# Reordering the start of an attention and expert kernel: casts, clamps, register loads, idle products and value rows

## The chip, the cores and the metric

One Trainium2 chip, one core. The metric is device time in microseconds (us), the median of several executions. An execution is "fast" when it lies within 1.5% of the fastest of its kernel; all the profiled executions quoted here were fast, and all ratios use fast runs only. Times inside an execution are counted from the start of the profiled span; the whole time is about 1.8 us more than the span (335.48 against 333.7 for the kernel before in its profiled execution).

## The reference, cut to what matters

```python
def _attn_ref(q, k, v, global_idx):              # float32, 8 batches x 8 heads x 576 tokens x 64
    scores = 1.0 / np.sqrt(D) * np.matmul(q, k.transpose(0, 1, 3, 2))
    mask = np.abs(pos[:, None] - pos[None, :]) <= 32
    mask = mask | is_global[:, None] | is_global[None, :]     # 8 global tokens, the same for all heads
    scores = np.where(mask, scores, -1e9)        # then softmax over the last axis
    return np.matmul(attn, v)

def _moe_ref(x, w_in, w_out):                    # x 4608x512, w_in 512x2048, w_out 2048x512
    r = np.maximum(x @ w_in, 0.0)
    return (r * r) @ w_out
```

Attention is a band of 65 tokens plus 8 "global" tokens that attend to everything and are attended by everything. Its result, one row per token, goes through two dense products.

## The kernel before: the parts that the change and the argument touch

Everything is placed by hand: in the trace an engine's instructions come in the order of the program text (VectorE's clamps at 6.74 to 7.85 us and its register load at 7.70 to 8.55, then the casts of head pair 1 from 8.63), so where a line stands decides what it holds up. Batch 0 is done in two halves of 288 query columns. Its first half (`half0`) needs casts, TensorE transposes and masks; its second half (`half1`) is mixed with the first products of the expert part ("projections", `mm1_half`). From batch 2 on the kernel is a steady mixture of attention and dense products.

```python
    def clamped(t, off, top):                    # two VectorE instructions on 8 numbers
        dve.tensor_scalar(out=t, in0=g32, scalar1=off, scalar2=0, op0=ALU.add, op1=ALU.max)
        dve.tensor_scalar(out=t, in0=t, scalar1=top, scalar2=None, op0=ALU.min)

    def columns():
        clamped(g32a, 0, HS)
        clamped(g32b, -255, S - 256)
    ...
    def fetch_globals():                         # SyncE: rows of the global tokens
        ...                                      # batch 0's v rows into gv0, then
        for nm in "kqv":                         # batches 1 and 2: k rows, q rows, v rows
            for g in range(NG):
                nc.sync.dma_start(out=grow[nm][g : g + 1], in_=...)

    def globals_in_place():
        for nm in "kq":
            act.copy(out=nat[nm][TP : TP + NG, :, TJ - 1], in_=grow[nm][:, 0])
        dve.tensor_copy(out=g16s["v"], in_=grow["v"])
        ...
    def value_globals(b):                        # SyncE: v rows of the global tokens into the value tile
        for x in range(NT):
            nc.sync.dma_start(out=vb[b][0:NG, x, 0 : 2 * H : 2], in_=...)

    def tokens_to_scratch(b):                    # GpSimd issues: batch b's k and q as fp16 rows in HBM
        for nm in "kq":
            ...
            for x in range(n):
                pool.dma_start(out=scr[(nm, b % 2)][...], in_=src[nm][b, :, lo:hi].rearrange("h s d -> s h d"))
    ...
    def scatter(b, part=None, pairs=slice(0, NHP)):   # the global tokens' outputs over their columns
        ...
        for g in range(NG):                      # the column comes from a VectorE register
            dve.tensor_copy(
                out=xT[:, pairs, lo:hi][:, :, ds(gvs[part][g], 1)],
                in_=gxs[b][:, pairs, g : g + 1],
            )
    ...
    # the order of the program's start
    cast_tokens(dve.tensor_copy, "k", 0)
    cast_tokens(act.copy, "q", 0)
    mask_natural(0)
    transposes0(0)
    mg = mask_globals_matmul(0)
    mask_globals(mg, 0)
    columns()                                    # clamps and a register load on VectorE,
    load_columns(0)
    cast_tokens(dve.tensor_copy, "k", 1)         # ahead of the casts of head pair 1
    cast_tokens(dve.tensor_copy, "q", 1)
    ...
    take(SCHED["h1"])                            # projections of the first half of the tokens
    half1(2)
    half1(3)
    ...
    half1_out(3)
    scatter(0, 1)                                # the second half's scatter
    take(99)
    globals_in_place()
    value_globals(1)                             # batch 1's v rows: only here
    globals_to_scratch(2)
    tokens_to_scratch(2)
```

In the steady part, after the first unit of batch b, GpSimd copies one number computed by that unit (`pin`, a brake so that the transfers do not start too early), on some batches gathers the global rows, then issues batch b+1's tokens to scratch; SyncE transposes them into `qb` and `kb`, which batch b+1's scores read.

The softmax here doesn't subtract the row's maximum and nothing guards it: scores larger than these inputs give would overflow.

## Time and profile before

| | kernel before |
|---|---|
| time, median of 3 runs | 335.12 us (334.07 to 335.83) |
| profiled span | 333.7 us |
| mean granted TensorE clock | 0.974 |
| TensorE busy from 75 to 290 us | 213.9 of 215.0 us |

Parts of the page of the kernel before. The first rows give busy us of an engine, its share of the span and its number of instructions; `PEclk` is the granted TensorE clock in tenths, for 40 equal slices of the span (8.3 us each).

```profile
span 333.7 us, 6906 instructions
...
PE 319.6 (96%) x2418; PEld 168.4 (50%) x2418; DVE 230.7 (69%) x681; ACT 211.4 (63%) x417; POOL 106.2 (32%) x137
...
PEclk9659988999999999999999999999999999999999
```

TensorE (PE) is busy 96% of the span, so a change must either take work from it, fill its last holes, or end the stretches at half clock: slices 2 and 3, and 6 and 7, are below 9.

Two more views of the kernel before matter for what follows; the prediction did not show them. First the instructions of one tile: VectorE's (DVE) scatter copies over the whole execution, with the least, median and greatest duration in ns. Then the order of time around the second half's scatter: start, length, engine, line, operation, output<-input, and in brackets what the engine waited for.

```profile
L729 DVE COPY xT<-gx x72: 170/177/814, 25.6 to 274.1; 128x4 f16 x72
```

```profile
33.70 3.65 POOL L405 DMA_DIRECT2D scr_k<-in_k_dram  x4
...
34.91 2.79 PE L528 MATMUL mm<-xT,w_in 128*128 128x256 f16 x24
...
36.54 2.45 DVE L729 COPY xT<-gx 128x4 f16 x8
...
38.23 0.76 POOL L405 DMA_DIRECT2D scr_k<-in_k_dram  x1 [0.88 <-DMA w_out<-in_moe_w_out_dram]
...
39.05 1.92 PE L528 MATMUL mm<-xT,w_in 128*128 128x256 f16 x16 [0.66 <-DVE xT L729]
```

A scatter copy takes 177 ns, but one of them took 814. Eight undisturbed ones take 1.66 us with the steps between them (measured further below); this scatter took 2.45. Its first copy, of 814 ns, runs from 36.54 to 37.35, beside GpSimd (POOL) still issuing four scratch copies, and its last, of 338 ns, beside the issue at 38.23. TensorE waits 0.66 us for the scatter.

### The profile page before, as it was taken

The page shows a single profiled execution, that of the slowest core. Times are in us where ns is not written, and L with a number is a line of the kernel's source. Part 1 is how long each engine was busy: PE and PEld are TensorE (multiplying, and loading weights), DVE is VectorE, ACT ScalarE, POOL GpSimd, SP SyncE. Part 2 cuts the span into 40 slices and gives each one's busy share as a digit, 9 for nine tenths or more (in the row PEclk, how much of TensorE's full clock was granted, in tenths as well). Part 3 has the DMA queues.
Part 4 walks back from the last instruction along what each step waited for, and adds up shares of the span by engine and source line. Part 5 has one row for each costly group of instructions (what it writes and reads, how often), then busy time and mean ns, then how long its engine had stood idle before and what let it go on. Part 6 is the DMA issues. An engine that isn't in the chain of part 4 may idle for free.

```text
span 333.7 us, 6906 instructions
## 1 busy us (share of the span) xinstructions
PE 319.6 (96%) x2418; PEld 168.4 (50%) x2418; DVE 230.7 (69%) x681; ACT 211.4 (63%) x417; POOL 106.2 (32%) x137
## 2 busy tenths in 40 slices
PE   7888879999999999999999999999999999999995
PEld 2676755444454555455455445454545444444443
DVE  7686976888858885878588858885888584323511
ACT  4487765659954995399549954995499537404600
POOL 9545653005930593059004940590000000000000
PEclk9659988999999999999999999999999999999999
DMA  8999999922999399979952999999510001011011
GB/s 194 179 203 180 203 172 144 138 97 47 132 152 151 83 120 151 165 111 136 156 113 72 110 143 140 163 146 134 119 65 0 33 31 64 2 66 60 3 63 63
DMA packets 148716, 37.59 MB, mean 113 GB/s; under 512 B 136658, under 2 KB 144202, under 8 KB 148682
## 3 DMA queue, kind: packets, MB, share of 16 engines
q0 software_dynamic: 105168, 17.93, 70.6%
q1 hardware_dynamic: 43368, 19.10, 29.9%
q8 instruction: 19, 0.31, 0.4%
q10 hardware_dynamic: 146, 0.13, 0.1%
q14 instruction: 15, 0.12, 0.1%
HBM read 37.31 MB, written 17.05 MB: 163 GB/s over the span
## 4 chain that ended last, share of the span: by engine, by line
PE 77%; DMA 7%; DVE 7%; SPq 3%; ACT 3%; issue 2%; DVEq 0%
PE mm L509 25%; PE mm L572 24%; PE tr L509 9%; PE tr L572 5%; DMA qb<-scr_q 4%; PE sc L657 3%; PE acc L657 3%; PE sc L612 2%; DVE xT L729 2%; SPq L356 2%; DMA vb<-g16sv 2%; PE mm L528 2%; PE acc L612 1%; DMA grows<-in_k_dram 1%; DVE xT L710 1%
## 5 line engine op out<-in xcount | busy, mean ns | idle before, releaser
L572 PE MATMUL mm<-w_out,gt 128*128 128x512 f16 x448 | 104.5, 379 | 0.0
L509 PE MATMUL mm<-xT,w_in 128*128 128x512 f16 x384 | 90.1, 379 | 0.4 <-DVE xT L729 0.3
L572 PEld LDWEIGHTS <-gt 128*128 128x128 f16 x560 | 52.5, 98 | 58.5
L509 PEld LDWEIGHTS <-w_in 128*128 128x128 f16 x512 | 47.5, 98 | 53.4 <-issue 0.5
L514 ACT ACTIVATE rl<-mm 128x512 f16<-128x512 f32 x96 | 54.7, 600 | 25.6 <-PE mm L509 25.0
L515 DVE TENSOR_TENSOR gt<-rl 128x512 f16<-128x512 f16 x128 | 52.2, 423 | 16.5 <-ACT rl L514 14.4
L621 ACT ACTIVATE et<-sc 128x880 f16<-128x880 f32 (+1 forms) x32 | 28.9, 903 | 46.8 <-PE sc L612 46.8
L624 DVE TENSOR_TENSOR et<-et,mask 128x880 f16<-128x880 f16 (+1 forms) x64 | 38.9, 614 | 24.6 <-ACT et L621 23.4
L113 POOL DMA_DIRECT2D vb<-in_v_dram x40 | 41.1, 1594 | 6.1 <-DMA w_in<-in_moe_w_in_dram 5.1
L509 PE MATMUL tr<-xT,w_in 128*128 128x512 f16 x128 | 33.0, 380 | 0.0
L549 DVE COPY ot<-mm 128x512 f32<-128x512 f32 (+1 forms) x29 | 19.7, 680 | 17.5 <-PE mm L572 15.8
L871 POOL COPY pin<-gsh 1x1 f32<-1x1 f32 x5 | 0.9, 177 | 95.4 <-DVE gsh L698 95.4
L710 DVE TENSOR_TENSOR xT<-sc,rec 64x288 f16<-64x288 f32 (+1 forms) x55 | 25.0, 455 | 7.2 <-ACT rec L681 6.1
L681 ACT ACTIVATE rec<-rec 128x288 f32<-128x288 f32 x64 | 28.3, 443 | 2.0
L621 ACT ACTIVATE et<-acc 128x880 f16<-128x880 f32 (+1 forms) x32 | 29.0, 907 | 0.9 <-PE acc L612 0.9
L657 PEld LDWEIGHTS <-vb 128*128 128x128 f16 x288 | 21.3, 98 | 12.6 <-issue 1.8
L405 POOL DMA_DIRECT2D scr_k<-in_k_dram x30 | 26.7, 1114 | 1.7 <-DMA w_out<-in_moe_w_out_dram 0.9
L710 DVE TENSOR_TENSOR xT<-acc,rec 64x288 f16<-64x288 f32 (+1 forms) x55 | 25.0, 455 | 3.2 <-ACT rec L681 0.6
L680 ACT ACTIVATE rec<-sc 64x288 f32<-64x288 f32 (+1 forms) x55 | 22.4, 406 | 7.1 <-PE sc L657 4.2
L405 POOL DMA_DIRECT2D scr_q<-in_q_dram x24 | 24.8, 1582 | 5.2 <-DMA w_out<-in_moe_w_out_dram 5.1
L572 PE MATMUL tr<-w_out,gt 128*128 128x512 f16 x112 | 25.3, 379 | 0.0
L680 ACT ACTIVATE rec<-acc 64x288 f32<-64x288 f32 (+1 forms) x55 | 22.2, 404 | 1.3 <-PE acc L648 0.3
(146 smaller groups left out, 310.1 us busy)
## 6 DMA issues: line engine op xcount, KB each, us to landing
out_dram<-ot SPq DMA_DIRECT2D x35, 256.0 KB
vb<-in_v_dram POOLq DMA_DIRECT2D x32, 120.0 KB, 10.0
scr_q<-in_q_dram POOLq DMA_DIRECT2D x24, 144.0 KB, 6.2
scr_k<-in_k_dram POOLq DMA_DIRECT2D x24, 120.0 KB, 4.6
w_in<-in_moe_w_in_dram POOLq DMA_DIRECT2D x4, 512.0 KB, 13.4
w_out<-in_moe_w_out_dram POOLq DMA_DIRECT2D x4, 512.0 KB, 9.9
natk<-in_k_dram POOLq DMA_DIRECT2D x3, 288.0 KB, 14.0
natq<-in_q_dram POOLq DMA_DIRECT2D x3, 288.0 KB, 11.2
```

The lines of the kernel that those rows point to most:

```text
L113: pool.dma_start(out=vb[b][NG : NG + KN[x], x, 2 * hs.start : 2 * hs.stop : 2], in_=v[b, hs, x * KT : x * KT + KN[x]].rearrange("h s d -> ...
L405: pool.dma_start(out=scr[(nm, b % 2)][x * pitch + off : x * pitch + off + hi - lo].rearrange("s (h d) -> s h d", d=D), in_=src[nm][b, :, l ...
L509: nc.tensor.matmul(ph, w_in[:, t, u * P : (u + 1) * P], xT[:, t, XOFF + c * TC : XOFF + (c + 1) * TC], start=(t == 0), stop=(t == NDM - 1),)
L514: nc.scalar.activation(out=rl, in_=ph, func=AF.Relu)
L515: nc.vector.tensor_tensor(out=gts[c][:, u, :], in0=rl, in1=rl, op=ALU.mult)
L572: nc.tensor.matmul(po, gts[c][:, f, m * P : (m + 1) * P], w_out[:, f, :], start=(f == 0), stop=(f == NFF - 1),)
L621: act.activation(out=et[:, :, 0:W], in_=sc[:, :, 0:W], func=AF.Exp, bias=0.0, scale=scale)
L624: dve.tensor_tensor(out=et[:, :, 0:W], in0=et[:, :, 0:W], in1=mask[:, MB[half] : MB[half] + W].unsqueeze(1).to_broadcast((P, 2, W)), op=AL ...
L657: nc.tensor.matmul(banks[e][:, o : o + w], vtf[:, t, vo : vo + P], et[:, e, so : so + w], start=(n == 0), stop=(n == nw - 1), skip_group_c ...
L680: act.activation(out=rec[r], in_=av[xs][rs, :, 0:GTOK], func=AF.Ln)
L681: act.activation(out=rec, in_=rec, func=AF.Exp, scale=-1.0)
L710: dve.tensor_tensor(out=xT[r, hp, x0 : x0 + HS].rearrange("p (k x) -> p k x", k=2), in0=av[x][r, :, 0:GTOK], in1=rec[r], op=ALU.mult,)
```

## The change

The intent: take small work on VectorE out of the way of head pair 1's casts; make each clamp one instruction; put idle products into TensorE's waits so that the clock stays up (without them its mean was 0.972 to 0.984, with them 0.990 to 1.000, measured below); fetch and place batch 1's value rows before TensorE needs them.

```diff
-SCHED = dict(wa=6, w0=6, w1=5, w2=3, w3=2, w4=1, ...)
+SCHED = dict(w5=2, w6=1, w7=2, wa=6, w0=6, w1=5, w2=2, w3=4, w4=0, ...)
...
-    def clamped(t, off, top):
-        dve.tensor_scalar(out=t, in0=g32, scalar1=off, scalar2=0, op0=ALU.add, op1=ALU.max)
-        dve.tensor_scalar(out=t, in0=t, scalar1=top, scalar2=None, op0=ALU.min)
+    def clamped(t, least, most, of=None):
+        dve.tensor_scalar(
+            out=t, in0=g32c if of is None else of, scalar1=least, scalar2=most,
+            op0=ALU.max, op1=ALU.min,
+        )
...
-        for nm in "kqv":
+        for nm in "vkq":
...
+    def values_in_place():
+        dve.tensor_copy(out=g16s["v"], in_=grow["v"])
+        value_globals(1)
...
-        act.copy(out=gv16, in_=gv0)
+        dve.tensor_copy(out=gv16, in_=gv0)
...
-    cast_tokens(act.copy, "q", 0)
+    cast_tokens(dve.tensor_copy, "q", 0)
+    transposes0(0)
+    cast_tokens(dve.tensor_copy, "k", 1)
+    cast_tokens(act.copy, "q", 1)
     mask_natural(0)
-    transposes0(0)
-    mg = mask_globals_matmul(0)
-    mask_globals(mg, 0)
-    columns()
-    load_columns(0)
-    cast_tokens(dve.tensor_copy, "k", 1)
-    cast_tokens(dve.tensor_copy, "q", 1)
...
     half0(0)
+    keep_warm(SCHED["w5"])
     half0(1)
...
+    columns()
+    load_columns(0)
     v_globals()
...
     take(SCHED["h1"])
+    values_in_place()
     half1(2)
...
+    globals_in_place()
     scatter(0, 1)
     take(99)
-    globals_in_place()
-    value_globals(1)
+    next_in_place()
     globals_to_scratch(2)
     tokens_to_scratch(2)
```

Cut here: the same row copies split into three functions, the clamps' new bounds (the index base is moved into the access pattern instead of being subtracted), two further `keep_warm` calls and the mask's globals placed behind head pair 1's transposes. The arithmetic of the result is unchanged.

More of the change, by code (lines that the diff above doesn't have):

```diff
@@ L42 @@
 MB = (0, 456)
-SCHED = dict(wa=6, w0=6, w1=5, w2=3, w3=2, w4=1, h0=0, w=4, h1=3, h2=2, h3=0, p0=0, p1=2, p2=2, b1=((2, 1, 2), (2, 1, 2), (1, 1, 2), (2, 0, 4)))
+SCHED = dict(w5=2, w6=1, w7=2, wa=6, w0=6, w1=5, w2=2, w3=4, w4=0, h0=0, w=4, h1=3, h2=2, h3=0, p0=0, p1=2, p2=2, b1=((2, 1, 2), (2, 1, 2), (1, 1, 2), (2, 0, 4)))
 ONES = 2.0**-7 * (1.0 + 15360.0 / 2**23)
@@ L197 @@
     gbf = sbt("gbf", [P, NG], FP32)
-    g32, g32a, g32b, g32c = (sbt("g32" + x, [1, NG], I32) for x in ("", "a", "b", "c"))
+    g32a, g32b, g32c = (sbt("g32" + x, [1, NG], I32) for x in "abc")
     oh = sbt("oh", [P, NT, NG], FP16)
@@ L206, in indices @@
         low = g64.bitcast(I32).rearrange("p (g two) -> p g two", two=2)[:, :, 0]
+        clamped(g32c, 0, S - 1, low)
         nc.vector.tensor_copy(out=g16, in_=low)
@@ L209, in indices @@
         nc.tensor.matmul(gb, ones, g16, start=True, stop=True)
-        nc.vector.tensor_copy(out=g32, in_=low)
-        clamped(g32c, 0, S - 1)
-        return gb
-    def clamped(t, off, top):
-        dve.tensor_scalar(out=t, in0=g32, scalar1=off, scalar2=0, op0=ALU.add, op1=ALU.max)
-        dve.tensor_scalar(out=t, in0=t, scalar1=top, scalar2=None, op0=ALU.min)
+        return gb
+    def clamped(t, least, most, of=None):
[3 more added lines that the diff above has]
+        )
     def columns():
         clamped(g32a, 0, HS)
-        clamped(g32b, -255, S - 256)
+        clamped(g32b, 255, S - 1)
     def one_hots(gb):
@@ L368, in globals_in_place, with next_in_place @@
             act.copy(out=nat[nm][TP : TP + NG, :, TJ - 1], in_=grow[nm][:, 0])
-        dve.tensor_copy(out=g16s["v"], in_=grow["v"])
+    def next_in_place():
         for nm in "kq":
@@ L717, in load_columns @@
     def load_columns(part):
-        idx, top = {None: (g32c, S - 1), 0: (g32a, HS), 1: (g32b, S - 256)}[part]
+        idx, low, top = {None: (g32c, 0, S - 1), 0: (g32a, 0, HS), 1: (g32b, 255, S - 1)}[part]
         _, gvs[part] = nc.values_load_multi_w_load_instructions(
-            idx[0:1, 0:NG], engines=[mybir.EngineType.DVE], min_val=0, max_val=top,
+            idx[0:1, 0:NG], engines=[mybir.EngineType.DVE], min_val=low, max_val=top,
             skip_runtime_bounds_check_because="the values are clamped on the chip",
@@ L725, in scatter @@
         lo, hi = {
-            None: (XOFF + b * S, XOFF + (b + 1) * S), 0: (0, HS + 1), 1: (XOFF + 255, XOFF + S),
+            None: (XOFF + b * S, XOFF + (b + 1) * S), 0: (0, HS + 1), 1: (XOFF, XOFF + S),
         }[part]
@@ L748 @@
     cast_tokens(dve.tensor_copy, "k", 0)
-    cast_tokens(act.copy, "q", 0)
+    cast_tokens(dve.tensor_copy, "q", 0)
+    transposes0(0)
+    cast_tokens(dve.tensor_copy, "k", 1)
+    cast_tokens(act.copy, "q", 1)
     mask_natural(0)
-    transposes0(0)
-    mg = mask_globals_matmul(0)
-    mask_globals(mg, 0)
-    columns()
-    load_columns(0)
-    cast_tokens(dve.tensor_copy, "k", 1)
-    cast_tokens(dve.tensor_copy, "q", 1)
     keep_warm(SCHED["w3"])
     tr_k(1, tail=act.copy, last=act.copy)
+    mg = mask_globals_matmul(0)
     keep_warm(SCHED["w4"])
     tr_q(1, act.copy)
+    mask_globals(mg, 0)
     ets = {}
@@ L792 @@
         pool.dma_start(out=w_out[:, ts(j, 4), :], in_=wo[:, ts(j, 4), :])
+    columns()
+    load_columns(0)
     v_globals()
     half0(2)
+    keep_warm(SCHED["w6"])
     half0(3)
+    keep_warm(SCHED["w7"])
     half0_out(0, "mm")
```

## The prediction

> **What bounds the kernel now.** I read the page's row of slices first, then the stretches between the changes of the granted TensorE clock, then the first 75 us instruction by instruction. In the stretches view a row gives start:end, length, then busy us of each engine with its instruction count, the granted clock, the DMA share and GB/s (all times here are us from the span's start):
>
> ```profile
> core 0: us, PE busy (x) PEld busy (x) DVE busy (x) ACT busy (x) POOL busy (x), PEclk, DMA share, GB/s
> 4.25:11.07 6.82, 4.43 (x69) 2.86 (x68) 5.81 (x25) 2.73 (x12) 6.75 (x8) 0.98 1.54 202
> 11.07:24.73 13.66, 12.20 (x222) 9.70 (x222) 9.93 (x39) 9.96 (x24) 6.17 (x8) 0.51 1.44 197
> 24.73:48.62 23.89, 20.41 (x254) 15.18 (x253) 19.38 (x52) 16.85 (x33) 12.98 (x16) 0.99 1.66 186
> 48.62:52.03 3.41, 3.39 (x28) 2.27 (x29) 1.14 (x4) 1.75 (x4) 3.41 (x5) 0.54 2.29 168
> 52.03:75.00 22.97, 22.46 (x244) 11.62 (x242) 18.73 (x68) 13.14 (x28) 0.68 (x1) 1.00 1.11 124
> 75.00:333.70 258.70, 253.69 (x1601) 125.83 (x1599) 173.34 (x480) 165.74 (x319) 72.72 (x84) 1.00 0.90 97
> ```
>
> From 75 us on TensorE is busy 253.7 of 258.7 us at the full clock, and the diff leaves that part alone. So the change is worth whatever it moves the point at 75 us, and no more. Before it TensorE runs at half clock twice, 11.07 to 24.73 and 48.62 to 52.03. "Busy" there means slow, not well used. The two causes are in the order of time, VectorE then TensorE:
>
> ```profile
> 6.74 0.15 DVE L215 TENSOR_SCALAR g32a<-g 1x8 int32<-1x8 int32 x1
> 6.92 0.16 DVE L216 TENSOR_SCALAR g32a<-g32a 1x8 int32<-1x8 int32 x1
> 7.00 0.65 DVE L215 TENSOR_SCALAR g32b<-g 1x8 int32<-1x8 int32 x1
> 7.69 0.16 DVE L216 TENSOR_SCALAR g32b<-g32b 1x8 int32<-1x8 int32 x1
> 8.63 0.56 DVE L435 CAST nat0k<-stk 96x768 f16<-96x768 f32 x1 [0.79 <-DVE g32b L216]
> 9.11 0.74 DVE L435 CAST nat0q<-stq 96x768 f16<-96x768 f32 x1
> ```
>
> ```profile
> 9.25 0.43 PE L453 MATMUL mm<-identity,nat0k 96*128 96x96 f16 x6 [1.97 <-DVE nat0k L435]
> ...
> 46.63 0.26 PE L648 MATMUL sc<-et,vb 128*64 128x160 f16 x2 [0.44 <-DVE gt L540]
> 46.70 0.26 PE L648 MATMUL sc<-et,one 128*64 128x160 f16 x2
> 48.02 0.27 PE L648 MATMUL sc<-et,vb 128*64 128x192 f16 x2 [1.05 <-DMA vb<-g16sv]
> 48.10 0.27 PE L648 MATMUL sc<-et,one 128*64 128x192 f16 x2
> 48.64 0.28 PE L648 MATMUL sc<-et,vb 128*64 128x88 f16 x2 [0.27 <-DMA vb<-g16sv]
> ```
>
> In the first, clamps and a register load stand in VectorE's queue ahead of the casts of head pair 1, and TensorE waits 1.97 us for them. In the second, batch 1's first output products wait for the global value rows that SyncE copies into the value tile. The 0.44 put down to VectorE is really the same DMA: by the semaphore updates the first row block landed at 46.5.[...]
>
> One reading to distrust: the chain of waits names the row DMAs and the cast gv between 13.39 and 18.58. By the semaphores those eight v rows had all landed at 14.8; ScalarE came to the cast at 17.94 because it works in order behind the copies of q.
>
> [...] 48.62 to 52.03 is 3.41 us, and the idle products cost 0.43 us each at 1.2 us and 0.25 at 4.0. [...] the five 8 KB row blocks issued from 41.20 on landed at 46.5 to 49.5, behind a share over 1. [...] a clamp of eight numbers costs 0.15 us here.
>
> **The change, part by part.** The order of instructions was compared for both kernels; TensorE gets 5 more idle products in all (4838 to 4848 rows with weight loads).
>
> *Start, to 5.9 us.* Clamp first, no g32 copy: SyncE's row loads begin about 0.5 us earlier (the clamp's end moves from 2.75 to 2.23), VectorE saves about 0.4 us of small operations. But gbf still waits for six idle products, so gbf at 4.10 and the cast of k0 at 4.54 stay. Worth 0 here.
>
> *Head pairs 0 and 1.* VectorE now does k0 4.54, q0 5.26, the copy of kt0 5.98, k1 6.55 to 7.1 (its data landed at 6.1), mask half 0 (0.92 us as before) to 7.95, the copy of kt1 to 8.6. ScalarE casts q1, whose data lands at 7.67, to 8.5 (0.83 us as its cast of q0 took). TensorE fills with four idle products, transposes k1 at 7.35 and q1 at 8.5 to 9.1. ScalarE then does kt1's tail, qt1 to 9.9 and the four mask pieces (0.54) that stood earlier before, so the first exponential starts at 10.3 against 11.36: 1.1 us won of the 1.97.
>
> *Head pairs 2 and 3.* The two exponentials end at 12.1, mask pieces at 12.6, VectorE's multiplications at 12.75, kt2 to 13.6. The third transpose group waits for the mask pieces' bank (12.6), the fourth for kt2 (13.6), so it ends at 14.2 against 17.28. Of these 3 us, 1.1 are the earlier start, the rest the clock: a group of 12 transposes and 12 products takes 0.77 cold and 0.55 or so warm, and before, TensorE reached them only at 13.92. Then VectorE: kt3 to 14.55, memset 0.27, two clamps 0.3, register load 0.8, the gv cast 0.55 (rows there by 14.8), so the five copies start near 16.5 against 18.58. That serial row is what the moved clamps and the moved cast cost: about 1.6 us of it are new on this path.
>
> *Outputs of half 0.* They start near 17.1 against 19.35. Warm, each takes 0.5 us instead of 0.95, but ScalarE's two activations a head (0.41 + 0.44, one head each 0.94 in the trace) pace this stage either way: first at 18.1 against 20.51, so the next exponential near 21.8 against 24.14. **Sum to here: 2.3 us.** The chain to 46 us (VectorE's scatters, projections) keeps its lengths: 2.3 carried along.
>
> *Batch 1's rows early.* The 0.68 us cast of g16sv moves from 40.50 to about 32.6 of the old clock. It displaces two multiplications that had 0.2 to 0.4 us to spare: 0.2 us lost. At 40.50 TensorE was dense, so taking it away there wins nothing. The row copies go out right after the last row fetch, and land by 40 at the worst, needed at 44. So TensorE does at 44.0 in 0.5 us what took from 46.19 to 48.96: 2.3 us won. And no half-clock window follows: 8 projections at 1.82 become 0.93, outputs at 0.87 become 0.45, together 1.3 us. VectorE, with 5.9 us of work in this unit of attention, gives back some: its multiplication at 55.45 moves to about 49.9, so I count 0.4 lost. **Sum: 2.3 - 0.2 + 2.3 + 1.3 - 0.4 = 5.3 us.**
>
> *ScalarE's copies of k and q rows.* Now ahead of the scatter and, since v rows go first, q rows land last, at 34.3 or so, while ScalarE is there at 33.9. A stall of half a us, with TensorE waiting for the scatter anyway: 0.
>
> **Rivals.** First, batch 2's data takes over. DMA is saturated to 64 us and does not get shorter: the transposes of q landed at 66.5, batch 2's value rows at 69.4; batch 2's scores started at 73.43 and its outputs at 75.85. So 6.9 and 6.4 us are there to be won before this binds; 5.3 fits, barely. It caps the gain: about 328.7. Second, the clock stays cold: between 11 and 17 us my TensorE is used only some 55 to 65% of the time, and if that is not enough a half-clock window may return. Where ScalarE paces, it costs 0; if it reaches the projections, up to 1.4 us: about 331.3. Third, the row of small VectorE work at 14.5 to 16.5 is longer than worked out (a clamp of 0.65 us is in the trace), and only 1 us of the first part is left: 331. Fourth, a worse wait: the scatter's or the SyncE queue's order turned against it, with nothing won: 335. Nothing in the trace speaks for this.
>
> **Range and chances.** 335.1 - 5.3 = 329.8. The rivals span 328.7 to 331.3; with 0.5 to 1 us of scatter of runs (334.07 to 335.83 before) I take 328.2 to 332.0. Faster by over 2% needs 6.7 us, which needs more than my sum and meets the first rival: 0.12. Slower by 2%: 0.01.
>
> **What would show it.** Right: the granted clock stays full past 11.07 and past 48.62; the gaps of 1.97 and 1.05 are gone; first exponential of batch 0 near 10.3, the fourth-half exponential near 21.8, batch 1's first outputs near 44, batch 2's scores near 68, and the part after it as long as before. Wrong: a half-clock window remaining in the first 25 us, a wait of batch 2 for the transposes of q or its value rows, VectorE's first copy of gv later than 17, or a long wait of ScalarE for q's rows. The most likely failing term is 2.3 for the first half, where I laid three engines' orders by hand.

## The result, and the profile after

| | before | after |
|---|---|---|
| time, median of 4 runs each | 335.21 us (334.07 to 335.83) | 332.18 us (331.87 to 332.45) |
| profiled span | 333.7 us | 330.6 us |
| mean granted TensorE clock | 0.974 | 0.995 |

The ratio is 0.9913, 95% interval 0.9884 to 0.9942: within 2%, and 3.0 us less. A ratio here is the mean time of one kernel's fast runs over that of the other's fast runs of the same rounds, so it is not quite the ratio of the medians in the table. Forecast were 5.3 us of gain and a time between 328.2 and 332.0.

The page of the changed kernel, the same rows:

```profile
span 330.6 us, 6920 instructions
...
PE 317.5 (96%) x2423; PEld 165.4 (50%) x2423; DVE 230.4 (70%) x678; ACT 210.5 (64%) x416; POOL 106.5 (32%) x137
...
PEclk9979999999999999999999999999999999999999
```

One slice is left below 9. The stretches of the prediction's first view, for the changed kernel (the last ends with its span):

```profile
core 0: us, PE busy (x) PEld busy (x) DVE busy (x) ACT busy (x) POOL busy (x), PEclk, DMA share, GB/s
...
4.25:11.07 6.82, 6.21 (x72) 3.54 (x71) 5.84 (x27) 3.14 (x14) 6.36 (x8) 1.00 1.49 200
11.07:24.73 13.66, 11.28 (x234) 7.39 (x234) 10.72 (x40) 9.22 (x23) 6.46 (x9) 0.88 1.45 196
24.73:48.62 23.89, 21.57 (x279) 16.87 (x278) 19.54 (x51) 17.64 (x36) 12.74 (x15) 1.00 1.65 189
48.62:52.03 3.41, 2.85 (x22) 1.12 (x20) 3.18 (x11) 2.51 (x4) 2.84 (x4) 1.00 2.40 157
52.03:75.00 22.97, 22.33 (x238) 11.86 (x238) 18.46 (x66) 14.22 (x30) 2.19 (x5) 1.00 1.18 137
75.00:330.60 255.60, 250.20 (x1577) 123.65 (x1575) 170.72 (x473) 162.51 (x313) 72.40 (x83) 1.00 0.90 97
```

The clock rose from 0.51 to 0.88 between 11.07 and 24.73 (what is left is one half-clock window, 20.23 to 23.64) and from 0.54 to 1.00 in the fourth stretch. So the clock did what was wanted. (By the trace the half-clock windows of the kernel before lie 0.26 us earlier than the stretches say, 10.81 to 24.46 and 48.36 to 51.77; nothing hangs on it.) To see where the time went, follow TensorE's milestones (start in us; the last column is how far ahead the changed kernel is):

| TensorE begins | before | after | ahead |
|---|---|---|---|
| scores of batch 0, head pair 0 | 10.40 | 9.84 | 0.56 |
| scores, head pair 2 | 17.21 | 14.72 | 2.49 |
| second half's scores, head pair 0 | 23.23 | 21.51 | 1.73 |
| first projections | 28.68 | 26.71 | 1.97 |
| second half's scores, head pair 2 | 31.41 | 29.43 | 1.97 |
| **projections of the second half** | 39.05 | 38.20 | **0.85** |
| scores of batch 1, head pair 0 | 43.14 | 42.29 | 0.85 |
| scores of batch 1, head pair 1 | 53.52 | 48.98 | 4.54 |
| scores of batch 2 | 73.43 | 70.00 | 3.43 |
| scores of batch 3 | 106.91 | 103.43 | 3.48 |
| scores of batch 4 | 140.95 | 137.88 | 3.07 |

The gain grows, falls from 1.97 to 0.85 at the second half's projections, jumps to 4.54 when the value rows are no longer waited for, gives 1.1 of that back before batch 2, and loses 0.4 more at batch 4. In the order of time around the fall, and for the same tile over the whole execution:

```profile
34.07 3.65 POOL L411 DMA_DIRECT2D scr_k<-in_k_dram  x4
...
34.59 3.55 DVE L735 COPY xT<-gx 128x4 f16 x8
...
38.20 1.92 PE L534 MATMUL mm<-xT,w_in 128*128 128x256 f16 x16 [2.09 <-DVE xT L735]
```

```profile
L735 DVE COPY xT<-gx x72: 170/177/864, 24.0 to 271.1; 128x4 f16 x72
```

The scatter now begins 1.95 us earlier than it did, as it should, but it takes 3.55 us instead of 2.45, and TensorE waits 2.09 us for it instead of 0.66. GpSimd's four issues begin at 34.07, against 33.70: the issues ahead of them wait for earlier transfers (the one at 32.21 for 0.68 us, until `natq` lands), so they did not move with the scatter. By the trace's records, the eight copies now take 414, 177, 669, 864, 378, 453, 177 and 178 ns; the last two start after 37.72, where the issues end, and are short again. The scatter has been moved into the issues.

The records show more: the copies of 414, 669, 864 and 453 ns end at 35.01, 35.92, 36.82 and 37.72, and the four issues end at 35.01, 35.92, 36.82 and 37.72. In the ten profiles here that have the scatter as copies, 38 copies took over 300 ns, all beside an issue; 32 of them end within 0.03 us of the end of an issue, and the other six part-way through a fourth issue in a row. None of the 649 copies with no issue beside it took over 190 ns.

The first half, in the order of time (VectorE's small work and the value copies that TensorE waits for):

```profile
15.48 0.26 DVE L214 TENSOR_SCALAR g32a<-g32c 1x8 int32<-1x8 int32 x1
15.56 0.19 DVE L214 TENSOR_SCALAR g32b<-g32c 1x8 int32<-1x8 int32 x1
...
17.07 0.41 DVE L448 CAST gv<-grows 8x512 f16<-8x512 f32 x1 [1.32 <-DMA grows<-in_v_dram]
17.52 0.48 DVE L450 COPY vb<-gv 8x512 f16<-8x512 f16 x2
...
17.85 0.26 PE L654 MATMUL mm<-et,vb 128*64 128x160 f16 x2 [1.31 <-DVE vb L450]
```

The bracket at 17.07 names a transfer, but those rows had landed at 15.0 by the semaphores; between 15.78 and 16.62 lies the register load in VectorE's queue (0.84 us, not counted as busy; in the kernel before this one, of `g32a`, took 0.85 us and that of `g32b` 0.61). TensorE pays for it with a wait of 1.31 us.

Batch 1's first output products, in the order of time, no longer wait for anything:

```profile
45.17 0.24 PE L654 MATMUL sc<-et,vb 128*64 128x160 f16 x2
...
45.31 0.25 PE L654 MATMUL sc<-et,vb 128*64 128x192 f16 x2
...
45.48 0.21 PE L654 MATMUL sc<-et,vb 128*64 128x88 f16 x2
```

And TensorE's waits between 66 and 142 us (us in total, times, longest), where the kernel before had 0.7 us for the same:

```profile
PE sc L618 <- DMA qb<-scr_q: 1.1, 1, 1.1
```

This wait is at the start of batch 4, whose transposed q landed at 137.74.

### The profile page after: what moved, and what is told of

Same layout as the page of the kernel before. It is cut to its first block, busy times and chain, and to the rows that moved or that the text cites. A ratio compares the mean times of both kernels' runs of the same rounds, so it can differ in the third digit from the quotient of the medians.

```text
span 330.6 us, 6920 instructions
## 1 busy us (share of the span) xinstructions
PE 317.5 (96%) x2423; PEld 165.4 (50%) x2423; DVE 230.4 (70%) x678; ACT 210.5 (64%) x416; POOL 106.5 (32%) x137
## 4 chain that ended last, share of the span: by engine, by line
PE 67%; DVE 9%; ACT 7%; SPq 6%; DMA 6%; issue 3%; ACTq 0%; DVEq 0%
PE mm L515 22%; PE mm L578 22%; PE tr L515 8%; PE tr L578 5%; DMA qb<-scr_q 4%; SPq L362 4%; PE sc L663 3%; PE acc L663 2%; DVE xT L735 2%; PE sc L618 2%; SPq L357 2%; DVE xT L716 2%; ACT rl L520 2%; DMA grows<-in_q_dram 1%; ACT et L627 1%
## 5 line engine op out<-in xcount | busy, mean ns | idle before, releaser
L630 DVE TENSOR_TENSOR et<-et,mask 128x880 f16<-128x880 f16 (+1 forms) x64 | 38.9, 614 | 25.1 <-ACT et L627 24.3
## 6 DMA issues: line engine op xcount, KB each, us to landing
vb<-in_v_dram POOLq DMA_DIRECT2D x32, 120.0 KB, 10.3
```

The lines of the kernel that those rows point to most:

```text
L630: dve.tensor_tensor(out=et[:, :, 0:W], in0=et[:, :, 0:W], in1=mask[:, MB[half] : MB[half] + W].unsqueeze(1).to_broadcast((P, 2, W)), op=AL ...
```

## The experiments

**Theory.** The missing 2 us go in good part to the second half's scatter (1.12 of 2.2, by the table above): VectorE's copies are held up while GpSimd issues transfers, and the change moves the scatter into those issues. **Rivals:** the gain of the value rows was smaller than worked out and moves along with the rest; the remaining half-clock window costs it; the register load in the first half costs it; later transfers (transposed q) take the gain back.

Twelve kernels were run, in three calls of four; each call shared its runs of the kernel before. All gave correct results. The column "call" tells which are to be compared directly. The medians are of all runs; all were fast but four of the 22 with the value rows late.

| kernel | call | median us (runs) | ratio to before, 95% interval | second half's scatter, us | batch 2's scores at |
|---|---|---|---|---|---|
| before | 1 / 2 / 3 | 334.89 (29) / 334.76 (54) / 334.87 (19) | | 2.45 (profile above) | 73.43 |
| changed kernel, control | 1 | 332.02 (8) | 0.9909, 0.9874 to 0.9943 | 3.38 | 69.51 |
| GpSimd brake, first try | 1 | 330.76 (6) | 0.9898, 0.9869 to 0.9926 | 2.59 | 68.74 |
| scatter as tensor_tensor | 1 | 330.06 (6) | 0.9858, 0.9830 to 0.9885 | 1.66 | 67.89 |
| value rows late again | 1 | 333.00 (22) | 0.9940, 0.9918 to 0.9962 | 3.22 | 73.17 |
| value rows early, alone | 2 | 332.79 (17) | 0.9941, 0.9918 to 0.9964 | 3.60 | 72.05 |
| no idle products in the waits | 2 | 332.57 (22) | 0.9939, 0.9919 to 0.9959 | 3.34 | 71.98 |
| tensor_tensor and load in the gap | 2 | 329.30 (6) | 0.9842, 0.9808 to 0.9875 | 1.66 | 66.63 |
| gathers hoisted | 2 | 334.02 (22) | 0.9980, 0.9958 to 1.0002 | 3.37 | 69.47 |
| GpSimd brake, mended | 3 | 330.08 (6) | 0.9860, 0.9823 to 0.9898 | 1.65 | 68.23 |
| before, scatter as tensor_tensor | 3 | 333.42 (14) | 0.9970, 0.9940 to 1.0001 | 1.66 | 70.89 |
| load in the gap alone | 3 | 329.35 (6) | 0.9845, 0.9799 to 0.9891 | 1.78 | 67.42 |
| all three, gathers behind | 3 | 328.17 (6) | 0.9805, 0.9766 to 0.9843 | 1.65 | 67.06 |

### The control

The changed kernel unedited.

> The changed kernel again, as the yardstick for the three runs beside it. Both theories: 332.2 us, scatter of half 1 (8 VectorE copies) about 3.5 us, batch 2's first scores near 70.0.

It came out at 332.02 us, 0.9909, as in the first comparison (0.9913), with a scatter of 3.38 us. The result and the long scatter repeat.

### Is it GpSimd's issues? A brake, first try

```diff
     globals_to_scratch(2)
+    pool.tensor_copy(out=pin[0:1], in_=xT[0:1, 0, XOFF : XOFF + 1])
     tokens_to_scratch(2)
```

The idea: GpSimd first reads a number that the scatter writes, so its issues begin only after the scatter.

> The changed kernel, but GpSimd issues batch 2's token copies only after the scatter of half 1. Collision theory: the scatter shrinks from 3.5 us to 1.7, projections after it start near 36.5 instead of 38.2, and the time falls by 1.1 to 1.7 us to about 330.8; the later issue costs nothing because the transfers ahead keep the queue full to 45. Rival (the scatter is slow by its own register work, or by the rows' landing): the scatter stays near 3.5 and the time at 332.2. Second rival (batch 2's data becomes late): scatter short, but batch 2's scores wait for the transposes.

```profile
34.02 0.75 POOL L797 DMA_DIRECT2D w_out<-in_moe_w_out_dram  x1 [0.63 <-issue]
34.29 2.59 DVE L735 COPY xT<-gx 128x4 f16 x8
...
34.77 0.18 POOL L842 CAST pin<-xT 1x1 f32<-1x1 f16 x1
34.90 3.56 POOL L411 DMA_DIRECT2D scr_k<-in_k_dram  x4
```

This was a miss of construction: the column read is not one that this scatter writes, so GpSimd did not wait, and its four issues began at 34.90, 0.61 us into the scatter. An issue of the output weights (34.02 to 34.77) already lay beside the first copy, which took 465 ns; the second was under way when the four began, and of the rest two took 522 and 457 ns. The scatter took 2.59 us against the control's 3.38. The copies that were held end where issues end (34.75, 35.75 and 36.66), which fits the theory and does not decide it.

### The same scatter by another operation

The theory can be tested without moving anything in time: the same copies as a product with a tile of ones. If only copies are held, the product will stay short beside the issues; if the issues slow any VectorE instruction, it will be as long as the copies were. The trace of the kernel before speaks for the first: the 128 products `gt<-rl` of its line 515 (128x512, fp16) took 411 to 427 ns, the 56 that lay beside one of GpSimd's direct issues (DMA_DIRECT2D) no longer than the other 72 (411 to 427 and 414 to 427). Why a copy should be held and a product not, no view here tells.

```diff
-            dve.tensor_copy(
+            dve.tensor_tensor(
                 out=xT[:, pairs, lo:hi][:, :, ds(gvs[part][g], 1)],
-                in_=gxs[b][:, pairs, g : g + 1],
+                in0=gxs[b][:, pairs, g : g + 1],
+                in1=one64[:, 0:NHP].unsqueeze(2), op=ALU.mult,
             )
```

> The changed kernel with each scatter copy made a two-input multiplication by one (same result). Collision theory[...]: the eight take about 1.7 us although GpSimd issues beside them, and the time falls by about 1.1 us to 331.1. Rival (GpSimd's issues slow any VectorE instruction, or SBUF traffic in general): still 3 us or more, time 332.2.

The order of time, and the tile over the whole execution:

```profile
34.12 3.64 POOL L411 DMA_DIRECT2D scr_k<-in_k_dram  x4
34.37 1.66 DVE L735 TENSOR_TENSOR xT<-gx,one 128x4 f16 x8
...
36.08 1.92 PE L534 MATMUL mm<-xT,w_in 128*128 128x256 f16 x16 [0.20 <-DVE xT L735]
```

```profile
L735 DVE TENSOR_TENSOR xT<-gx,one x72: 168/177/179, 23.8 to 269.7; 128x4 f16 x72
```

The scatter lies wholly beside the same four issues (34.12 to 37.76) and takes 1.66 us; none of the 72 instructions exceeds 179 ns, where the longest copy took 864. TensorE waits 0.20 us instead of 2.09. Nothing else differs in the program, so it is the copy form beside GpSimd's issues that is slow: this settles the theory. (The runs show that the form and the neighbour decide, 864 ns against 179 at the longest; the reason behind it they do not show.) The scores of batch 2 begin at 67.89, 5.54 us ahead of before, near the 5.3 that the prediction had summed for that point, and the time is 330.06 us, where the prediction was 329.8. That closeness is in part luck: this scatter of 1.66 us is also 0.8 shorter than the 2.45 of before, which the prediction had carried along unchanged.

### GpSimd's brake, mended

The same brake with a column that the scatter does write.

```diff
-    pool.tensor_copy(out=pin[0:1], in_=xT[0:1, 0, XOFF : XOFF + 1])
+    pool.tensor_copy(out=pin[0:1], in_=xT[0:1, 0, XOFF + S - 1 : XOFF + S])
```

> What x3 was meant to be: the changed kernel, GpSimd's wait now on the last columns that the scatter of half 1 writes, so no issue of batch 2's token copies runs beside it (one issue of the output weights may). Collision theory: scatter 1.7 to 2.2 us, projections of half 1 near 36.5, 1.1 to 1.7 us less than the changed kernel: about 330.6. Rival (slow by itself): 3.4 us still.

```profile
34.54 1.65 DVE L735 COPY xT<-gx 128x4 f16 x8
...
36.26 0.30 POOL L842 CAST pin<-xT 1x1 f32<-1x1 f16 x1 [2.17 <-DVE xT L735]
36.51 4.40 POOL L411 DMA_DIRECT2D scr_k<-in_k_dram  x5
```

Copies again, but with GpSimd made to wait: 1.65 us. The time is 330.08 us. One way leaves the overlap and changes the form of the copies, the other keeps the form and takes the overlap away; both give the same scatter and the same time. Batch 2's data, issued 2.4 us later (36.51 against 34.07), was not missed: between 56 and 72 us no wait for a transfer is listed. So the first rival of the prediction, that batch 2's transfers bind, does not show here.

### Value rows: taken out, and alone

Out of the changed kernel:

```diff
-        for nm in "vkq":
+        for nm in "kqv":
...
-    values_in_place()
     half1(2)
...
     take(99)
+    values_in_place()
     next_in_place()
```

> The changed kernel with the value rows of batch 1 cast and placed late, as before, and fetched in the old order; the first half stays reordered. My theory: it keeps the first half's 2.0 us up to the scatter, loses about 1 of them there, meets the wait for the rows and the half-clock window again: 334.2 us, so the rows are worth 2 to 2.7 us. Rival (the first half carries the gain): 333 or less, with no half-clock window near 48.

It took 333.00 us against the control's 332.02, not the 334.2 expected: the rows cost 1 us here, and the number is the rival's. In its profile batch 2 began at 73.17, so that nearly all of the lead was gone, and two stretches at half clock were back (17.5 to 24.3 and 48.2 to 51.6). But that execution took 334.69 us at a mean clock of 0.982, and 16 of the 22 runs had 0.987 or more: it is not typical. Nor are the 3.66 us between the two profiles (69.51 and 73.17) the rows' alone: the first half-clock stretch lies long before any value row is placed, and the first projections already began at 27.31 instead of 26.71.

And alone, on the kernel before (row order "vkq" and the early placing, nothing else):

> The kernel before with one part of the change: batch 1's v rows fetched first, cast and placed before half 1's last two heads. My theory: the wait of 2.3 us and the half-clock window at 48 go, about 1 us is lost at the scatter or on VectorE: 332.6 us. Rival (the rows' early copies cost VectorE and SyncE as much as they win): 334.5 or more. The first 28 us as before, batch 2's first scores near 71.

332.79 us, 0.9941: some 2.0 us of gain by this part alone, with a scatter of 3.60 us, longer than the 2.45 of before. The half-clock window near 50 us was gone, the first one still there (11.84 to 25.49). So the rows alone gain 2.0 us, and the change without them also gains 2.0 (0.9940), where both together gain 3.0: the parts do not add up, and neither is shown to be the larger. The rows' kernel too loses a microsecond in the scatter.

### The kernel before with the other scatter

The same replacement of the copies, in the kernel before.

> The kernel before with the scatter copies as two-input multiplications, nothing else. The collisions there cost 0.36 us (2.02 against 1.66) in the first scatter and 0.8 (2.45 against 1.66) in the second. Collision theory: both 1.66, TensorE's first projections of half 1 up to 1.1 us earlier, but the wait for the value rows that follows takes it back: within 0.5 us of before, 334.5. Rival (the rows' wait moves along): 333.7.

The second half's projections began at 38.03 instead of 39.05, and the first scatter took 1.65 instead of 2.02. So the kernel before paid for the collision too, about 1 us of it; its time fell by about that (0.9970, an interval that just includes 1). The expectation that the wait for the rows would take it back was wrong; the number is the rival's. The waits before batch 1's first output products stayed about as long (0.56, 0.37 and 0.68 us against 0.44, 1.05 and 0.27), but the half-clock window near 50 us did not come, so that batch 2's scores began at 70.89, 2.5 us earlier. That is one profile, and more than the timed runs show. What can be said is that the collision was already in the trace of before and worth about 1 us there, 2 us in the changed kernel (332.02 to 330.06).

### The idle products in the waits

The idle products `w2` to `w7` set to 0 in the changed kernel: those that it adds, and the six that the kernel before had in these places too.

> The changed kernel without any of the idle products in batch 0's first half after the one-hots (w2 to w7 all 0). If the removed waits alone keep the clock up: 332.0 as the changed kernel, full clock from 6.8 to 18. If the products do it: a half-clock window or two between 10 and 24, but ScalarE and VectorE pace that stage, so at most 1 us: 332.0 to 333.0.

The clock fell to half in 11.44 to 25.09 and 38.75 to 42.16, and the first projections began at 27.27 instead of 26.71. The time is 332.57 us, 0.9939, against 0.9909 for the control in another call: 0.3 percentage points (1 us), with intervals that overlap. All 22 of its runs had a mean clock of 0.972 to 0.984, the control's eight 0.990 to 1.000. So the idle products do keep the clock up, and that clock is worth about 1 us, not clear of noise. That it is so little because ScalarE and VectorE pace the first half is argued, not tested.

The window that the change left (20.23 to 23.64) can be judged from two other profiles. The first brake and the hoisted gathers (below) have the same program up to the scatter, and no half-clock window at all there; their first projections began at 26.40 and 26.36, against 26.71 here and 26.39 in the control, which had the window. So it costs 0.3 us at most.

### The register load, moved into a wait

After the change VectorE waits 1.13 us for the first exponential. The clamps and the load go there:

```diff
     mask_natural(1)
+    columns()
+    load_columns(0)
     half0(0)
...
-    columns()
-    load_columns(0)
     v_globals()
```

First together with the tensor_tensor scatter:

> The run x4 (scatter as a two-input multiplication) with the two clamps and the register load moved to where VectorE waits 1.1 us for the first exponential. If that row of small work set the time of gv: gv starts near 15.7 instead of 17, first projections near 25.3 instead of 26.5, and 1.2 us less than x4: 328.9. If ScalarE or VectorE after it paces the stage anyway: gv earlier but first projections at 26.3 or later, time as x4, 330.1.

The load ran at 10.9 us, the cast of the value rows at 15.30 instead of 17.07, the first projections at 25.10 instead of 26.71, and no slice of the page's clock row is below 9 (nor is one in the first brake's, without this edit). 329.30 us, 0.9842; the scatter's change alone had 0.9858 in another call, so in time little of the 1.3 us that the profiles show at batch 2 (66.63 against 67.89) is sure.

Then alone, with the copies as they were, to separate the two:

> The changed kernel with the clamps and the register load moved into VectorE's wait, the scatter as copies. gv near 15.5, first projections near 25.3, so 1.2 us won there as in x8; but the scatter of half 1 now starts near 33.1, while GpSimd issues from 33.3 to 37.7, so the collision gives most of it back: first projections of half 1 near 37.7 as in the changed kernel, time 331.5 to 332. Rival (no collision): near 37.0, 330.8.

```profile
33.22 1.78 DVE L735 COPY xT<-gx 128x4 f16 x8
...
33.84 0.75 POOL L799 DMA_DIRECT2D w_out<-in_moe_w_out_dram  x1 [0.56 <-issue]
34.59 3.64 POOL L411 DMA_DIRECT2D scr_k<-in_k_dram  x4
```

This expectation failed, and taught something. The scatter was expected to stay long; it took 1.78 us. Being 1.37 us earlier, it was over at 35.00, and had most of its copies behind it when the four issues began at 34.59 (0.5 us later than in the changed kernel's profile, which helped). Beside the issue at 33.84 it had three copies, of which only the last was held, for 302 ns, to the issue's end. The loss is a matter of where the scatter falls against GpSimd's issues, and a register load moved elsewhere, 20 us before, can end it. The time, 329.35 us (328.14 to 331.91), is therefore not the worth of the register load alone.

### The wait for transposed q

The scatter's cure gained 5.54 us at batch 2's start, but its batches 3 and 4 then waited 1.8 us for transposed q (0.7 in the kernel before), and the whole gained 4.8 by the ratio. Batch b+1's rows start only when GpSimd has copied `pin` in batch b; in batches 2, 3 and 5 three gathers stand ahead of them in GpSimd's queue. First, on the changed kernel otherwise as it is, the six gathers of batches 2 and 3 put ahead of the loop:

```diff
+    gather(0)
+    gather(1)
     for b in range(2, B):
...
-                if b == 2 or b % 2:
+                if b == 5:
```

> The changed kernel with the gathers of global rows for batches 3 and 4 issued ahead of batch 2's loop instead of after each batch's first unit. Theory of the data loop: from the first unit of batches 2 and 3 to the landing of the transposed q takes as long as a batch, so TensorE waits about 1 us there; gathers off that loop make the data about 4 us earlier, those waits go to 0, and the time falls by about 1 us to 331. Rival (a transfer's noise, not the loop's length): waits for the transposed q stay near 1 us and the time at 332.

The wait for q went (it had landed at 134.45, batch 4's scores began at 139.09), but the time rose to 334.02 us. Six gathers between 71.5 and 79.0 held `pin` back to 78.97, and batch 2's second and third units together took 2.9 us longer than in the changed kernel's profile (19.64 against 16.69); TensorE's waits in that stretch are put down to VectorE's weights:

```profile
PE sc L663 <- DVE et L630: 2.1, 2, 1.8
```

Why VectorE and ScalarE stood idle for about 2 us there, this profile does not show; that stays open.

Then, with the scatter and the load as above, one gather ahead of the loop and the others behind the issues that matter:

```diff
+    gather(0)
     for b in range(2, B):
...
-                if b == 2 or b % 2:
-                    gather((b - 1) // 2)
...
                 values(b + 1)
+                if b in (2, 4):
+                    gather(b // 2)
                 value_globals(b + 1)
```

> x8 with the gather for batch 3 ahead of batch 2's loop (three issues, not six) and the one for batch 4 behind batch 3's values. Data loop theory: no wait for the transposed q at batches 3 and 4 (x8 had about 1.0 us in both), the time 0.5 to 1 us under x8: 328.5. If three gathers disturb batch 2's second unit as six did in x9: 1 to 2 us lost there, 330 or more.

No wait for q is left (it landed at 98.36 for scores at 100.45, and at 128.92 for scores at 133.71). 328.17 us, 0.9805, the best of all, about 4 us under the changed kernel (0.9909 to 0.9805, in different calls). How much of it the gathers brought is open: the wait differs between executions (1.1 and 1.2 us in the two profiles of the changed kernel), and the load in the gap alone, with the gathers where they were, had none either. In the same call this kernel is 1.2 us below that one, which has copies for the scatter besides. Between 75 and 290 us TensorE is then busy 214.6 of 215.0 us.

## Why the prediction was right or wrong

The prediction named 5.3 us and got 3.0; its range ended at 332.0 and the time was 332.18. By its own terms, in the profiles:

| term | predicted | measured |
|---|---|---|
| first half of batch 0 (to the first projections) | 2.3 | 1.97 (1.72 at the exponential of the second half, to which the prediction summed: 22.42, not 21.8) |
| "The chain to 46 us (VectorE's scatters, projections) keeps its lengths: 2.3 carried along." | 0 | -1.12 (1.97 to 0.85) |
| value rows, clock after them, minus what VectorE gives back | 3.0 | 2.58 (0.85 to 3.43) |
| from batch 2 on | 0 | -0.36 (3.43 to 3.07) |
| sum | 5.3 | 3.07 |

**The step that failed is the sentence on the scatters.** It assumed that an instruction keeps its length when it is moved. The scatter did not, because GpSimd's issues, which hang on transfers, stayed where they were, and the scatter moved from the end of the four (0.8 us of overlap) to their middle (3.1 us). It took 3.55 us instead of 2.45, which is the 1.1 us lost in the table, half of the 2.2 that were missing in all. The fourth rival came near, "the scatter's or the SyncE queue's order turned against it", and was dismissed with "Nothing in the trace speaks for this". The trace did speak: a scatter of 2.45 and one of 2.02 us where eight copies of 177 ns need 1.66, and a copy of 814 ns beside an issue. The two experiments that take away the collision give 330.06 and 330.08 us, inside the range; they win 2 us and not 1.1 because they also remove what the kernel before had paid.

**First half: right in kind, 0.3 too large.** The clock's first window went, as named, though a later one (20.23 to 23.64) came in its place, as the second rival had feared; it cost 0.3 us at most. VectorE's small row, which the third rival warned of, was longer: the cast began at 17.07 and the first copy at 17.52 (16.5 was worked out), where "VectorE's first copy of gv later than 17" was to be the sign of error. The first exponential came at 11.01 and not 10.3, but with 2.49 won at head pair 2 that was not the path. A group of 12 transposes and 12 products, put at 0.77 us cold and 0.55 warm, took 0.80 at the clock of 0.50 (14.74 to 15.54 in the kernel before) and 0.45 at 1.00 (12.77 to 13.22 in the changed one). SyncE's row loads began at 3.65 against 3.74, not 0.5 us earlier; this cost nothing.

**Value rows: right.** The wait and the half-clock window after it are gone: 3.69 us won between 0.85 and 4.54 (3.4 summed). That the window would go with the wait was the author's estimate, and not shown in general: in the kernel before with the other scatter the waits stayed and the window near 50 us did not come. What VectorE gives back is 1.11 us instead of 0.4: TensorE now waits 0.56, 0.22 and 0.22 us for VectorE's `xT` at 49.90, 57.19 and 63.43. ScalarE's copies of the k and q rows cost nothing visible, as predicted.

**The first rival was right in kind and wrong in place.** The transfers were dense as it says: the page's DMA row is 8999999922 for the first ten slices of the kernel before and 8999999936 for the changed one, so at 90% or more from 8.3 to 66 us in both. Data did take something back, but not batch 2's: batch 4's transposed q, 1.1 us of wait instead of 0.7. The loop from `pin` over the gathers and scratch to `qb` (107.71 to 137.74) is as long as what is left of a batch after its first unit, so an earlier start of the batches does not shorten it. It is not of one length, though: with the load in the gap alone batch 4 began without a wait 29.0 us after its `pin`. With the gain of the scatter in, the wait was 1.8 us in one profile and 0.5 in another (the mended brake); with the gathers reordered it was gone, but so it was in one profile without that, so that the remedy is not shown.

**The range was too narrow.** It allowed for the known rivals and 0.5 to 1 us of scatter of runs, and nothing for an instruction that changes its length.

## What to carry to other kernels

When work is moved, ask not only what it waits for but what will run beside it: instructions whose durations in the trace spread (177 to 814 ns for one shape) are the ones to suspect, and their neighbours on the other engines can tell why: here the slow ones end where a neighbour ends. A VectorE copy on the critical path beside GpSimd's DMA issues can be written as a product with ones, or GpSimd can be made to wait; both were worth 2 us here. After each microsecond won at the start, look at the loops that a data transfer closes (brake, gather, scratch, transpose), because they need not get shorter with it: here the loop still took 30.0 us (107.71 to 137.74) after `pin` had come 3.5 us earlier (111.19 to 107.71).

## What the traces show of the held copies and of the clock

- The copies are held up by GpSimd's DMA issues: 177 ns undisturbed, as much as 864 in a stretch of four issues of 3.65 us together.
- The product of two tensors was not held: 72 of 72 took 168 to 179 ns, eight of them beside the same issues.
- A DMA issue did not hold the copies for its whole length. In the kernel before, copies of 177 ns each began at 38.23 and 38.45 inside an issue (38.23 to 38.99), and the next, at 38.66, was held to that issue's end (338 ns); with the load in the gap alone, copies of 177 and 176 ns began at 33.85 and 34.06 inside an issue (33.84 to 34.59), and the next, at 34.27, was held to that issue's end; in the changed kernel's fourth issue in a row (36.47 to 37.72) one copy was let go at 37.23 and the next held to 37.72. So an issue held copies up in parts of its length, and twice in the fourth. (The ends of the copies and the issues agree to 0.03 us, but the profile's legend calls its spans on GpSimd rough.)
- The half-clock stretches last 3.41 us (20.23 to 23.64 in the changed kernel), twice that (17.5 to 24.3 with the value rows late) or four times (10.81 to 24.46 in the kernel before). The 3.41 us before a fall were not idle: TensorE was busy 1.55 and 1.92 us of them in the kernel before and 2.16 in the changed one. The windows are not fixed by the program alone: the same start has one in the control (18.80 to 22.21) and none in the first brake's profile.
